# An FFT filter and a low-rank mixer on one core: x loaded as 128 partitions in runs of eight rows, chunk and natural stores in one DMA

## The chip, the cores and the metric

The kernel runs on one core of a Trainium2 chip. The metric is the device time of one execution in microseconds; lower is better. The core has five engines that run their own instruction streams and meet at semaphores: PE (matmuls; its weight loads are shown as PEld), DVE, ACT and POOL (element work), and SP, which here only issues DMAs. DMAs are moved by 16 DMA engines that all queues share. POOL issues on a software queue (q0 in the profile), SP and ACT on hardware queues (q1 and q10).

## The reference

```python
def _attn_ref(x, filt_r, filt_i):            # x: (8, 3136, 256) f32; filt: (1569, 256)
    X = np.fft.rfft(x, axis=1)
    Y = X * (filt_r + 1j * filt_i)[None]
    return np.fft.irfft(Y, n=x.shape[1], axis=1)

def _moe_ref(x, U, V, w_ch1, w_ch2):         # U: (3136, 32), V: (32, 3136)
    h = x.transpose(0, 2, 1) @ U @ V
    u = x + h.transpose(0, 2, 1)
    ch = np.maximum(u @ w_ch1, 0.0) @ w_ch2  # 256 -> 1024 -> 256
    return u + ch
```

The second takes the first's output as its x. Eight batches are independent of each other.

## The kernel before

**The transform.** A sequence of 3136 rows is taken as 64 x 49: row index = 49 q + r, with q from 0 to 63 (`NQ`) and r from 0 to 48 (`NR`). The first transform runs over q, on PE, with the constant matrix `w64` (two copies of a 64 x 64 block on the diagonal), so that partitions 0 to 63 handle one set of r and partitions 64 to 127 another. The 49 values of r are therefore held in 25 columns of two halves (`NH = 25`; the second half has 24). Which r stands in which half and column is a list, `r` in `_consts`: blocks of four, first half 0-3, 8-11, ..., second half 4-7, 12-15, .... A chunk of x (`CH = [8, 8, 9]` columns, `load_x`, L147 to L163) is a tile `xt` of 128 partitions, cast from f32 to f16 by the DMA. The second transform runs over r, with the table `t2` (its rows in the order of that list), then comes the product with the filters (`ft`), then the inverse over r with table `g12`, and the inverse over q.

**The stages of a batch.** Batch 0 stays in SBUF (`first_f1`, `first_a`, `first_mid`). The other seven go through DRAM twice: `f1_units` (L451 to L470) multiplies a chunk by `w64` into `asb` (L460, L466) and stores it to `c1[b]` (L470); `load_a` (L480, on SP) reads it back by frequency; `forward`, `product` and `i1` (in `stream`) do the second transform, the products (DVE, and the sum on POOL, L523) and the inverse over r, and store to `c2[b]`; `load_e` reads that back as `e2`. `make_u` forms u with the low-rank part, `mm1` and `mm2` are the two channel matmuls. A group is 4 columns of one batch, that is 8 rows r of 64 q.

**Outputs.** In batches 0 and 1 and in the last two groups of the last batch the result is evicted with positions on the partitions (`out_natural`, L733) into an `och` tile (2 buffers) and stored by L743, on POOL, in the last batch on SP. From batch 2 on it is evicted channel-major and turned by DVE (`out_turned`, L774, L775) and stored by eight DMAs (L783), four on SP and four on POOL. Every second batch an odd column is stored by L738.

**The order.** The order is written by hand: groups run one after another, each has eight slots, a batch has 48 (`SB`), and `put` places the units of the other stages into slots. For batches above 3 chunk c of x is loaded at slot t0 - 72 + 12c and its first transform unit comes at t0 - 54 + 12c, where t0 is the slot of the batch's first product; `load_a` of a batch stands at t0 - 14. Each engine runs its instructions in the order in which they were issued. POOL's queue holds x loads, c1 stores (batch 1's are on SP), POOL's part of the output stores, the sums of the products, and at the start the filters, tables, V and weights. POOL's DMAs take eight semaphores in turn, so that each waits for the landing of the eighth DMA before it. `xt` has five buffers.

Of the kernel before, what the change touches and what calls it, by code (L numbers as in the profile page):

```python
# [13 lines left out]
SEQ = 3136  # L14
NQ, NR = 64, 49
NS = 32
DM = 256
RANK = 32
ESC = 16.0
NH = 25  # L20
CH = [8, 8, 9]
# [5 lines left out]
def _consts():  # L27
    n, half = SEQ, SEQ // 2
    r = np.array([8 * (k // 4) + 4 * h + k % 4 for h in range(2) for k in range(NH - h)])
    q = np.arange(NQ)  # L30


    w = np.zeros((NQ, NS, 2))
    for s in range(NS):
        w[:, s, 0] = np.cos(2 * np.pi * s * q / NQ)
        w[:, s, 1] = -np.sin(2 * np.pi * s * q / NQ)
    w[:, 0, 1] = (-1.0) ** q
    w = w.reshape(NQ, 64)
    turn = np.arange(64).reshape(4, 16).T.ravel()
    w64 = np.zeros((128, 128))  # L40
    w64[:64, :64] = w
    w64[64:, 64:] = w
    s2 = np.zeros((128, 128))
    s2[:64, :64] = w.T / ESC
    s2[64:, 64:] = w.T / ESC


    t2 = np.zeros((NS, 98, 128))
    g = np.zeros((NS, 128, 98))
    for s in range(NS):  # L50
        for j in range(49):
            if j < 25:
                f = s + 64 * j
                e, sg = np.exp(-2j * np.pi * f * r / n), 1.0
            elif s:
                f = 64 * (j - 24) - s
                e, sg = np.exp(-2j * np.pi * (n - f) * r / n), -1.0
            else:
                f = 32 + 64 * (j - 25)
                e, sg = np.exp(-2j * np.pi * f * r / n), 1.0  # L60
            ei = np.conj(e)
            if s:
                t2[s, :49, j], t2[s, 49:, j] = e.real, -e.imag
                t2[s, :49, 64 + j], t2[s, 49:, 64 + j] = sg * e.imag, sg * e.real
                g[s, j] = np.concatenate([ei.real, ei.imag]) * 2
                g[s, 64 + j] = np.concatenate([-ei.imag, ei.real]) * 2 * sg
            else:
                o = 0 if j < 25 else 49
                t2[s, o:o + 49, j] = e.real
                t2[s, o:o + 49, 64 + j] = e.imag  # L70
                g[s, j, o:o + 49] = ei.real * (2 if f else 1)
                g[s, 64 + j, o:o + 49] = -ei.imag * 2

    t2[0, :, 64] = 0
    t2[0, 49:, 64] = (-1.0) ** r
    g[0, 64] = 0
    g[0, 64, 49:] = (-1.0) ** r
    g *= ESC / n
    gs = np.concatenate([g[:, 64:], g[:, :64]], 1)
    f16 = np.float16  # L80
    return (w64.astype(f16), s2.astype(f16), np.eye(128).astype(f16),
            np.tile(np.eye(32), (4, 4)).astype(f16),
            np.pad(np.hstack([w[:, turn], w[:, turn].T / ESC]), ((0, 64), (0, 0))).astype(f16),
            np.ascontiguousarray(t2.reshape(4, 8, 98, 128).transpose(0, 2, 1, 3)).astype(f16),
            np.ascontiguousarray(g.reshape(4, 8, 128, 98).transpose(0, 2, 1, 3)).astype(f16),
            np.ascontiguousarray(gs[0:8].transpose(1, 0, 2)).astype(f16))
# [3 lines left out]
def kernel(  # L90
# [11 lines left out]
    nc = tc.nc  # L102
# [10 lines left out]
    RD = NR * DM  # L113
    c1 = [nc.dram_tensor(f"c1_{b}", (64, RD), F16, kind="Internal") for b in range(nb)]
# [8 lines left out]
    def bank(tag, name):  # L123
        return ps.tile([128, 512], F32, tag=tag, bufs=BUFS[tag], name=name)

    c0 = np.cumsum([0] + CH).tolist()
    st = [dict() for _ in range(nb)]

    def span(lo, hi):

        for h in range(2):
            yield h, (h * NH + lo) * DM, (min(hi, NH - h) - lo) * DM

    def rows(ap, b, r, n):

        return bass.AP(tensor=ap.tensor, offset=ap.offset + (b * SEQ + r) * DM,
                       ap=[[RD, NQ], [1, n * DM]])

    def natural(ap):

        return ap.rearrange("p (r i h a) -> p r h i a", i=4, h=2, a=32)

    def split(ap):

        return ap.rearrange("p (r h i a) -> p r h i a", i=4, h=2, a=32)

    def load_x(b, c, parts=None):  # L147
        if c not in st[b].setdefault("x", {}):
            st[b]["x"][c] = sb.tile([128, 9 * DM], F16, tag="xt", bufs=5, name="xt")
        t = st[b]["x"][c]  # L150
        for lo, hi in parts or ((c0[c], c0[c + 1]),):
            for h in range(2):
                m = (hi - lo) // 4
                nc.gpsimd.dma_start(  # L154
                    t[64 * h:64 * h + 64, (lo - c0[c]) * DM:(lo - c0[c] + 4 * m) * DM]
                    .rearrange("p (m e) -> p m e", m=m),
                    bass.AP(tensor=x.tensor, offset=x.offset + (b * SEQ + 2 * lo + 4 * h) * DM,
                            ap=[[RD, NQ], [8 * DM, m], [1, 4 * DM]]))
            if hi == NH:
                o = (NH - 1 - c0[c]) * DM  # L160
                if b:
                    nc.gpsimd.memset(t[64:128, o:o + DM], 0.0)
                nc.gpsimd.dma_start(t[0:64, o:o + DM], rows(x, b, NR - 1, 1))  # L163
# [6 lines left out]
    t2 = cst.tile([98, NS * 128], F16)  # L170
# [62 lines left out]
    for c in range(1, len(CH)):  # L233
        load_x(0, c)
# [28 lines left out]
    for h in range(2):  # L263
# [3 lines left out]
                    ap=[[64 * 1024, 4], [1024, 32], [1, 1024]]))  # L267
# [183 lines left out]
    def f1_units(b, both):  # L451
        ne = 0
        for c in range(len(CH)):
            xt = st[b]["x"].pop(c)
            asb = sb.tile([128, 9 * DM], F16, tag="asb", bufs=2, name="asb")
            for n0 in range(0, CH[c], 2):
                w = min(2, CH[c] - n0) * DM
                k = 64 if c0[c] + n0 == NH - 1 else 128
                pf = bank("o" if b == 1 else "m", "pf")
                nc.tensor.matmul(pf[:, 0:w], w64[:, :], xt[:, n0 * DM:n0 * DM + w],  # L460
                                 start=True, stop=True)
                dst = asb[0:k, n0 * DM:n0 * DM + w]
                if both and (ne % 2 if b > 1 else ne > 3 and ne not in (5, 7, 12)):
                    nc.vector.tensor_copy(dst, pf[0:k, 0:w])
                else:
                    nc.scalar.copy(dst, pf[0:k, 0:w])  # L466
                ne += 1
                if n0 + 2 >= CH[c]:
                    for h, o, n in span(c0[c], c0[c + 1]):
                        (nc.sync if b == 1 else nc.gpsimd).dma_start(c1[b].ap()[:, o:o + n], asb[64 * h:64 * h + 64, 0:n])  # L470
                yield


# [254 lines left out]
    def out_natural(gx, rr):  # L728

        b, r0, nr = groups[gx]  # L730
        po, och = pos[gx], ochs[gx]
        a = (rr - rr % 2) * DM
        nc.vector.tensor_copy(natural(och[:, a:(rr + 1) * DM]), split(po[:, 0:(rr + 1) * DM - a]))  # L733
        if rr < nr - 1:
            return
        eng = nc.gpsimd if b < nb - 1 else nc.sync
        if nr == 1:
            eng.dma_start(bass.AP(tensor=out.tensor,  # L738
                                  offset=out.offset + ((b - 1) * SEQ + NR - 1) * DM,
                                  ap=[[SEQ * DM, 2], [RD, NQ], [1, DM]]), och[:, 0:DM])  # L740
        else:
            for h in range(2):
                eng.dma_start(rows(out, b, 2 * r0 + 4 * h, 4), och[64 * h:64 * h + 64, 0:nr * DM])  # L743

    def evict(gx, a):

        if gx < 0 or a >= groups[gx][2]:
            return
        if turned(gx):
            if a % 2:  # L750
                out_turned(gx, a)
        elif a % 2 or a == groups[gx][2] - 1:
            out_natural(gx, a)
# [57 lines left out]
    for h in range(2):  # L811
        nc.gpsimd.tensor_copy(split(w2)[:, :, h], natural(w2n)[:, :, h])
    fill = f1_units(1, True)
    vgen = u_units()
    first_mid(fill)
# [18 lines left out]
    for k, t in enumerate(steps):  # L834
        put(t, mid)
        b, m = divmod(k - LAG, NP)
# [8 lines left out]
    for b in range(1, nb):  # L845
        for gi in range(NS // KG):
            t = steps[NP * (b - 1) + GP * gi]
            put(max(2, t - (14 if b > 3 else 9 + b // 3)), one(load_a, b, gi))
        if b > 1:
            fill = f1_units(b, b == 2)  # L850
            t0 = steps[NP * (b - 1)]
            for k in range(NF):
                put(4 + 1.1 * k if b == 2 else 18 + 2.8 * k if b == 3 else t0 - 54 + 3 * k, fill)
            for c in range(len(CH)):
                if b > 2 or c > 0:
                    put(6 * c - 5 if b == 2 else 9 + 8 * c if b == 3 else t0 - 72 + 12 * c, one(load_x, b, c))
# [58 lines left out]
```

## Time and profile before

| | |
|---|---|
| median of 3 runs | 534.28 us (533.61 to 538.67) |
| the profiled execution | 534.16 us, span 532.4 us |
| PE / DVE / ACT / POOL busy | 498.4 / 400.7 / 377.7 / 290.9 us |
| granted PE clock, mean | 0.988 |
| x loads (L154) | 46 of 256 KB, median 6.7 us to landing; 4 of 128 KB, 3.9 us |
| c1 stores (L470) on POOL | 30 of 256 KB, 4.9 us; 6 of 288 KB, 3.7 us |
| natural output stores (L743) on POOL | 24 of 256 KB, 4.9 us |
| mean DMA rate | 177 GB/s |

The profile is of one execution. Times in it count from the start of its span. "Issue to landing" runs from the instruction that issues a DMA to its last completion step. Sizes of the x loads are those of the f16 that is written; twice as much is read.

### The profile page before, as it was taken

What the parts mean: (1) busy time and instruction counts of PE and PEld (TensorE: products, weight loads), DVE (VectorE), ACT (ScalarE), POOL (GpSimd) and SP (SyncE); (2) the same over time, 40 slices, a digit from 0 to 9 for tenths busy, and PEclk for the clock granted to TensorE, in tenths of its full rate; (3) what the DMA queues carried; (4) which work ended last, traced back from release to release, by engine and by line L of the source; (5) the groups of instructions that cost most, each with busy time, mean ns of one, the idle gap of its engine ahead of it and who ended that gap; (6) DMA issues with size and microseconds to landing.
All of it is one profiled execution on the core that took longest, in us unless ns stands there. A gap on an engine that the chain in (4) does not pass through costs nothing.

```text
span 532.4 us, 11368 instructions
## 1 busy us (share of the span) xinstructions
PE 498.4 (94%) x4022; PEld 303.0 (57%) x4022; DVE 400.7 (75%) x574; ACT 377.7 (71%) x771; POOL 290.9 (55%) x412
## 2 busy tenths in 40 slices
PE   3877799999999999999999999989999999999995
PEld 3765266667667785555555555545555555454444
DVE  7897367757786758898998888978999877445663
ACT  2767756677678868888788878877777678765541
POOL 7797633345656456586677665765756564313000
PEclk9979989999999999999999999999999999999999
DMA  8989998986988577897989798896887575544324
GB/s 127 193 150 188 204 211 210 217 223 147 232 234 214 141 154 221 208 229 171 225 204 220 195 240 205 177 235 145 199 194 148 126 180 128 140 96 80 78 66 104
DMA packets 118426, 93.98 MB, mean 177 GB/s; under 512 B 52977, under 2 KB 100786, under 8 KB 118370
## 3 DMA queue, kind: packets, MB, share of 16 engines
q0 software_dynamic: 21936, 41.91, 38.3%
q1 hardware_dynamic: 93226, 49.75, 37.7%
q10 hardware_dynamic: 3208, 1.61, 1.1%
q8 instruction: 31, 0.51, 0.4%
q14 instruction: 25, 0.20, 0.1%
HBM read 56.25 MB, written 48.17 MB: 196 GB/s over the span
## 4 chain that ended last, share of the span: by engine, by line
PE 79%; DVE 6%; POOL 6%; DMA 6%; issue 2%; ACT 1%; DVEq 0%; POOLq 0%; ACTq 0%
PE phh L694 27%; PE po L765 21%; PE po L720 8%; PE px L499 5%; PE pi L535 5%; PE pu L620 4%; DVE uv L520 3%; PE pf L460 3%; DMA xt<-in_x_dram 3%; PE ph L577 2%; POOL low L284 2%; DVE uv L518 1%; DMA vq<-in_moe_V_dram 1%; DMA g<-gd 1%; POOL xt L154 1%
## 5 line engine op out<-in xcount | busy, mean ns | idle before, releaser
L702 ACT ACTIVATE h<-phh 128x512 f16<-128x512 f32 (+1 forms) x391 | 205.9, 578 | 71.8 <-PE phh L694 66.9
L694 PE MATMUL phh<-ut,w 128*128 128x512 f16 x768 | 197.6, 379 | 0.6 <-ACT h L702 0.3
L523 POOL TENSOR_TENSOR y<-uv 128x512 f16<-128x512 f16 x96 | 111.0, 1158 | 110.6 <-DVE uv L520 74.8
L765 PE MATMUL po<-h,w 128*128 128x512 f16 x560 | 143.8, 379 | 0.0
L520 DVE TENSOR_TENSOR uv<-px,ft 64x512 f16<-64x512 f32 x192 | 132.1, 688 | 2.6
L694 PEld LDWEIGHTS <-w 128*128 128x128 f16 x832 | 78.5, 98 | 77.2 <-issue 2.4
L518 DVE TENSOR_TENSOR uv<-px,ft 128x512 f16<-128x512 f32 x96 | 65.3, 680 | 42.1 <-PE px L499 35.8
L783 POOL DMA_DIRECT2D out_dram<-och x120 | 70.2, 592 | 42.9 <-DVE och L775 35.6
L539 ACT CAST esb<-pi 98x512 f16<-98x512 f32 x112 | 66.0, 589 | 36.9 <-PE pi L535 33.9
L765 PEld LDWEIGHTS <-w 128*128 128x128 f16 x560 | 51.6, 98 | 53.2 <-issue 1.1
L774 DVE TENSOR_TENSOR tt<-po,ut 128x512 f32<-128x512 f32 x70 | 48.4, 692 | 33.8 <-PE po L765 30.9
L720 PE MATMUL po<-w,h 128*128 128x256 f16 x448 | 58.9, 275 | 0.0
L499 PE MATMUL px<-a,t 98*128 98x256 f16 x256 | 50.0, 277 | 7.2 <-DVE uv L520 3.7
L775 DVE STREAM_TRANSPOSE och<-tt 128x512 f32<-128x512 f32 x70 | 49.8, 711 | 2.4
L466 ACT CAST asb<-pf 128x512 f16<-128x512 f32 (+1 forms) x79 | 45.7, 578 | 5.3 <-PE pf L460 4.2
L720 PEld LDWEIGHTS <-h 128*128 128x128 f16 x448 | 42.8, 98 | 10.8 <-issue 1.4
L507 DVE TENSOR_TENSOR uv<-px,ft 128x1024 f16<-128x1024 f32 x32 | 38.0, 1219 | 13.9 <-PE px L499 13.4
L499 PEld LDWEIGHTS <-t 98*128 98x128 f16 x256 | 23.0, 99 | 33.9 <-DVE uv L520 11.5
L535 PE MATMUL pi<-y,g 128*98 128x256 f16 x192 | 36.7, 271 | 2.0 <-POOL y L523 2.0
L684 ACT CAST ut<-pu 128x512 f16<-128x512 f32 x70 | 38.1, 610 | 0.0
L460 PE MATMUL pf<-xt,w 128*128 128x512 f16 (+1 forms) x91 | 33.4, 373 | 3.3 <-DMA xt<-in_x_dram 3.0
L535 PEld LDWEIGHTS <-g 128*98 128x98 f16 x256 | 29.6, 123 | 4.0 <-issue 2.1
(96 smaller groups left out, 445.0 us busy)
## 6 DMA issues: line engine op xcount, KB each, us to landing
xt<-in_x_dram POOLq DMA_DIRECT2D x46, 256.0 KB, 6.7
a<-c SPq DMA_DIRECT2D x28, 384.0 KB
e<-c SPq DMA_DIRECT2D x56, 192.0 KB
out_dram<-och SPq DMA_DIRECT2D x160, 64.0 KB
c<-esb SPq DMA_DIRECT2D x24, 384.0 KB
c<-asb POOLq DMA_DIRECT2D x30, 256.0 KB, 4.9
out_dram<-och POOLq DMA_DIRECT2D x120, 64.0 KB, 3.2
out_dram<-och POOLq DMA_DIRECT2D x24, 256.0 KB, 4.9
```

The lines of the kernel that those rows point to most:

```text
L499: nc.tensor.matmul(px[:, sl * DM:(sl + 1) * DM], t2[:, s * 128:(s + 1) * 128], a2[:, (2 * ml + sl) * DM:(2 * ml + sl + 1) * DM], start=Tru ...
L518: nc.vector.tensor_mul(uv[:, 0:512], px[:, :], ft[:, a:a + 512])
L520: nc.vector.tensor_mul(uv[p:p + 64, 512:1024], px[q:q + 64, :], ft[q:q + 64, b:b + 512])
L523: nc.gpsimd.tensor_add(y, uv[:, 0:512], uv[:, 512:1024])
L535: nc.tensor.matmul(pi[0:98, sl * DM:(sl + 1) * DM], g12[:, g:g + 98], y[:, o:o + DM], start=(fi == 0), stop=(fi == nf - 1), skip_group_che ...
L539: nc.scalar.copy(split(esb[:, ml * 512:(ml + 1) * 512]), natural(pi[0:98, :]))
L694: nc.tensor.matmul(pm[:, 0:w], w1[:, dh * 1024 + t * 128:dh * 1024 + (t + 1) * 128], ut[:, dh * w:(dh + 1) * w], start=(dh == 0), stop=(dh ...
L702: nc.scalar.activation(h[:, 0:w], pm[:, 0:w], RELU)
L720: nc.tensor.matmul(po[:, o:o + DM], hs[gx, t][:, rr * 128:(rr + 1) * 128], w2[:, t * DM:(t + 1) * DM], start=(t == 0), stop=False, skip_gr ...
L765: nc.tensor.matmul(po[:, :], w2[:, t * DM + dh * 128:t * DM + (dh + 1) * 128], hs[gx, t][:, :], start=(t == 0), stop=(t == 7))
L775: nc.vector.transpose(och.rearrange("p (j h a) -> p h j a", h=2, a=32)[:, dh], tt.rearrange("p (j t) -> p j t", t=32))
L783: (nc.gpsimd if k and b < nb - 1 else nc.sync).dma_start(dst, och[32 * i:32 * i + 32, k * 512:(k + 1) * 512] .rearrange("p (r e) -> p r e" ...
```

## The change

`load_x` issues one DMA for a chunk of 128 partitions in place of two of 64. To make both halves of the tile one access pattern, the first half takes rows 0-7, 16-23, ... and the second 8-15, 24-31, ..., so that a partition reads one run of eight rows (8,192 bytes) in place of two runs of four. The forward table `t2` gets its rows in that order (`rf`); the inverse table keeps the old order. The c1 stores and the natural output stores of a chunk or group, two DMAs of 64 partitions so far, become one of 128. The DRAM side of all three has the dimensions (2, 64, n). The single last row of chunk 2 keeps a DMA of its own, in the load and in the store. Batch 0's first chunk is still loaded in two parts of four columns.

```diff
+    rf = np.array([16 * (k // 8) + 8 * h + k % 8 for h in range(2) for k in range(NH - h)])
...
+            fe = f if sg > 0 else n - f
+            e = np.exp(-2j * np.pi * fe * rf / n)
+            ei = np.exp(2j * np.pi * fe * r / n)
...
-    t2[0, 49:, 64] = (-1.0) ** r
+    t2[0, 49:, 64] = (-1.0) ** rf
...
-            for h in range(2):
-                m = (hi - lo) // 4
-                nc.gpsimd.dma_start(
-                    t[64 * h:64 * h + 64, (lo - c0[c]) * DM:(lo - c0[c] + 4 * m) * DM]
-                    .rearrange("p (m e) -> p m e", m=m),
-                    bass.AP(tensor=x.tensor, offset=x.offset + (b * SEQ + 2 * lo + 4 * h) * DM,
-                            ap=[[RD, NQ], [8 * DM, m], [1, 4 * DM]]))
+            n = min(hi, NH - 1) - lo
+            nc.gpsimd.dma_start(
+                t[:, (lo - c0[c]) * DM:(lo - c0[c] + n) * DM],
+                bass.AP(tensor=x.tensor, offset=x.offset + (b * SEQ + c0[c] + lo) * DM,
+                        ap=[[8 * DM, 2], [RD, NQ], [1, n * DM]]))
...
-                    for h, o, n in span(c0[c], c0[c + 1]):
-                        (nc.sync if b == 1 else nc.gpsimd).dma_start(c1[b].ap()[:, o:o + n], asb[64 * h:64 * h + 64, 0:n])
+                    eng, n = nc.sync if b == 1 else nc.gpsimd, min(8, CH[c]) * DM
+                    eng.dma_start(bass.AP(tensor=c1[b], offset=c0[c] * DM,
+                                          ap=[[NH * DM, 2], [RD, 64], [1, n]]), asb[:, 0:n])
+                    if CH[c] > 8:
+                        eng.dma_start(c1[b].ap()[:, (NH - 1) * DM:NH * DM], asb[0:64, n:n + DM])
...
-            for h in range(2):
-                eng.dma_start(rows(out, b, 2 * r0 + 4 * h, 4), och[64 * h:64 * h + 64, 0:nr * DM])
+            eng.dma_start(bass.AP(tensor=out.tensor, offset=out.offset + (b * SEQ + 2 * r0) * DM,
+                                  ap=[[4 * DM, 2], [RD, NQ], [1, 4 * DM]]), och[:, 0:nr * DM])
```

## The prediction

> **What bounds the kernel now.** I read the page's engine totals first, then the chain of work that ended last, then the DMA issues. PE is busy 94% of a span of 532.4 us; the other engines have air on average.
>
> ```profile
> span 532.4 us, 11368 instructions
> PE 498.4 (94%) x4022; PEld 303.0 (57%) x4022; DVE 400.7 (75%) x574; ACT 377.7 (71%) x771; POOL 290.9 (55%) x412
> ```
>
> So a DMA costs something only where PE ends up waiting for it. The chain in order of time (start, length, what) shows where that happens already: its DMA pieces of over 3 us all lie in the first 66 us, and two of the five are loads of x, which the change rewrites.
>
> ```profile
> 6.13 6.56 DMA xt<-in_x_dram
> ...
> 19.55 5.63 DMA g<-gd
> 28.50 3.10 DMA ft<-in_filt_r_dram
> 39.57 6.76 DMA vq<-in_moe_V_dram
> ...
> 58.70 7.32 DMA xt<-in_x_dram
> ```
>
> The question is then how long one of the new transfers takes. The DMA view from 38 to 56 us (issues, KB each, median us to landing) holds the nearest relative of the new access pattern:
>
> ```profile
> xt<-in_x_dram POOLq DMA_DIRECT2D x4, 256.0 KB, 6.7
> w<-in_moe_w_ch_dram POOLq DMA_DIRECT2D x2, 256.0 KB, 11.4
> ```
>
> Same queue, same bytes, same cast from f32, but the `w1` loads (L264) take 11.4 us against 6.7. Their DRAM side has a leading dimension of 4, (4, 32, 1024), against 128 SBUF partitions. The trace's completion records say why: each DMA reports 16 steps, one an engine. Those of an x load come together (41.1 to 42.5 us). Of the first `w1` load 12 come at 45.0 to 47.8 and four at 51.7 to 52.2: four engines carried its bytes, the others had nothing to do. The small `a` load (L480, two partitions) on SP also shows only two late steps.
>
> **The new transfers.** The x loads, the c1 stores and the natural output stores become DMAs whose DRAM side is (2, 64, n), where the two strides can't be merged: 8 rows against 49 rows times 64. By the `w1` row I take it that two engines carry each. This trace shows no such DMA of 128 partitions, so the bounds are 16 engines below (rival A) and two above. (The Trainium skill, DMA: Bandwidth & Descriptors, "Why a DMA increments its semaphore by 16 and not by 1", says that the number of engines is the largest up to 16 that divides the slowest dimension of both patterns: two here. By it the sum stays as below; the four of `w1` agree.)
>
> Price of an x chunk: the packet records give 172 ns in the median for a 2,048 B packet that reads 4,096 B of f32. A chunk is 128 runs of 8,192 B, so 64 an engine: 64 x 2 x 172 = 22.0 us. The fixed part is 2.0 us (the first load of the run is issued at 1.3 and completes at 4.0, with four packets in between). So **24 us** instead of about 7; at the mean of these packets between 205 and 340 us, 210 ns, it is 29. I take 24 where the queues are empty, 26 later. Several chunks can be under way on different pairs of engines.
>
> Price of a c1 store or a natural store of 512 KB: 64 x 172 ns = 11.0, with 2.5 for issue and landing 13.5 us, against 4.7 and 4.9; 16 at the packets' mean later on.
>
> **Start, through batch 2 (+55.8).** Batch 0's four x loads are issued at 1.3 to 5.2 us, so the last lands at 5.2 + 24 = 29.2 instead of 15.2. The first transform ends 1.8 us after that, as now. The filters and tables behind it share the two engines and POOL's waits for earlier DMAs, and are 14 late too; their own backlog (t2's first part takes 5.5 us to land now) is gone, so I take +12.5.
> x(1,0), issued at 32.6 + 12.5, lands at 69.1; PE reaches it at 40.7 + 12.5 = 53.2: a wait of 15.9, total 28.4. V, `w1` and `w2` queue behind the batch's chunks; x(1,2) lands at 73.5, so POOL's `low` copies move from 46.4 to 73.7 (+27.3), in step.
> x(2,0), 51.8 + 27.3, lands at 103.1, wanted at 59.5 + 28.4: a wait of 15.2, total 43.6. x(2,1), 58.1 + 27.3, lands at 109.4, wanted at 66.2 + 43.6: nothing. x(2,2) stands on POOL behind the c1 store of x(2,0), so is issued at 65.3 + 43.6 and lands at 132.9, wanted at 77.1 + 43.6: a wait of 12.2, total 55.8.
>
> **Batches 3 to 7 (+68).** From the issue (L154) and the first matmul on the chunk (L460) the leads are: batch 3: 17.8, 20.8, 25.8 us; 4: 22.0, 21.8, 18.1; 5: 19.8, 16.2, 16.3; 6: 16.5, 16.6, 16.4; 7: 19.1, 16.2, 16.7. Against 26 almost all are short. PE runs in order, so the chunk's first matmul holds everything. But POOL issues the second and third chunk of a batch shortly before PE reaches the one ahead (265.7 against 268.4), so a wait for one lengthens the next one's lead. Carried on in this way the waits are 5.2, 0 (batch 3, whose first chunk has batch 2's waits to hide in); 4.0, 0.2, 7.7; 6.2, 3.6, 6.1; 9.5, 0, 9.6; 6.9, 2.9, 6.4: 68 us. At 24 the same gives 50, at 29 it gives 95.
>
> **c1 store to `a` load (+25).** SP's `a` load (L480) waits for the last c1 store of its batch. The first load takes 6.1 us to land (61.8 to 67.9). From that store's issue to the first product of the batch there are now 18.9, 18.0, 14.1, 15.2, 13.7 and 14.7 us in batches 2 to 7; needed are 13.5 + 6.1 = 19.6: short by 0.7, 1.6, 5.5, 4.4, 5.9, 4.9, together 23; 32 at a store of 15 us. Batch 1's three stores are on SP, and if they share one pair they take 33 us in a row, which ends about when the late batch 2 chunk lets PE go on: 2 at most. Behind the waiting `a` load SP's output stores are late as well, and their buffers have 10 us to spare.
>
> **Outputs (+16, and +8 at the end).** Natural stores of batches 0 and 1: an `och` buffer is written again 9.4 to 20.7 us after its store; 13.5 us overshoot at two places, 6 us in all (0 to 20). Turned stores on POOL keep their form, but a part of each sits behind a chunk on its two engines, and POOL itself waits when the eighth DMA before has not landed: both end when the chunk does, where PE mostly waits anyway; 10 (0 to 30). At the end the one store of 512 KB follows the last full copy at 526.7: 526.7 + 0.5 + 2 + 11 = 540.3 instead of 532.4, so 7.9. Nothing hides it.
>
> **The clock (+15).** After PE's idle stretch of 2.4 us up to 29.2 the granted clock is half for 6.9 us (the view of stretches; after the busy times stand the clock, 0.51, DMA share and GB/s):
>
> ```profile
> 28.40:35.30 6.90, 6.00 (x53) 5.32 (x54) 6.76 (x8) 3.71 (x11) 6.82 (x12) 0.51 0.78 132
> ```
>
> Some 14 waits are longer than that; each may cost up to 3.4 us of PE, partly paid back by a longer lead for the next chunk: 15 (0 to 40).
>
> **What it saves.** 25 issues of x, 14 c1 stores and 13 output stores at 0.61, 0.55 and 0.54 us: about 30 us of POOL and SP. POOL is busy 55% and its longest waits are for DVE's products, so it frees nothing that PE waits for; at the start the second load goes out 1 us sooner and is lost in the 24. The reordered table (`rf`) changes constants only, the matmuls keep shape and count: 0.
>
> **Sum.** 532.4 + 55.8 + 68 + 25 + 16 + 7.9 + 15 = 720.1. The profiled execution took 534.16 for its span of 532.4, and the median of the runs is 534.28: with 1.8 outside the span **722 us**.
>
> **Rivals.**
> A, the other side: the new DMAs run on all 16 engines. Then a chunk's single DMA lands in about 5 to 7 us, and the saved issues shorten the start by the 1 us by which the second load is earlier, perhaps 3 with the x load at 58.7 on the chain: 530 to 535. It decides if the pattern is spread by its 128 rows and not by the leading 2; the output stores of the odd rows (also 128 rows, 4.4 us) do so, but their two strides merge into one. The four late steps of `w1` speak against it. (The Trainium skill, same page, "Rules for kernel authors", advises one 128-partition transfer instead of two over disjoint halves; that would be this rival, and no run of the trace before shows it.) 5%.
> B, two engines, but the slack hides the middle: POOL, held up less, issues its chunks earlier (by their slots the lead of batches 4 to 7 is 18 slots of about 1.3 us, 23 us), and the `a` loads overlap these waits. Then start, end and little else: 532 + 56 + 8 + 10 to 35 + 2 = 608 to 633. For it: POOL's lag of 7 us behind its slots is its own. Against: 23 is still below 26. 12%.
> C, two engines and a pile-up: contention with SP's queue makes a chunk 29 us or more, stores block POOL and y comes late. Start with four exposed loads 5 longer, 76, then 95 + 32 + 20 + 30 + 8 + 30: 825. 13%.
> Forecast: 70%.
>
> **Chances and range.** A comparison here can't tell a change of under 1% from none. Faster by over 1%: 2% (part of A). Within 1%: 3%. Slower: 95%. The low end takes 24 us in the middle (50), 15 for the `a` loads, no side costs, and 15 off for chunks that POOL issues earlier: 532 + 56 + 50 + 15 + 8 - 15 + 2 = 648, and I go a little into B, 640. The high end is near C's, 810.
>
> **What would show it.** Completion steps of an x load: 14 early, two some 20 us later; landing of xt about 24, of c1 stores about 13, of the last store about 13. PE idle before L460 by about 110 us in all, and half clock after it. Packets of x twice as large, half as many. If xt lands in under 10 us, the count of engines is wrong and with it everything; if it lands in 24 but PE's waits at L460 stay near the start's, B.

## The result and the profile after

The changed kernel takes **793.99 us** in the median of 6 runs (787.18 to 799.1), the kernel before 533.63 us in 6 runs beside it (530.93 to 538.67): a ratio of **1.4847 [1.4755, 1.494]**. The forecast was 722 us with a range of 640 to 810. The profiled execution took 795.25 us for a span of 793.5 us, 261.1 us more than the span before.

In the profile after, L454 is the first transform (L460 before), L464 the c1 store, L477 the `a` load (L480 before), L484 the `e` load (L487 before), L496 the second transform's matmul (L499 before), L739 and L780 the natural and the turned output stores. The page's totals and its row of granted clock:

```profile
span 793.5 us, 11290 instructions
PE 546.4 (69%) x4022; PEld 322.0 (41%) x4022; DVE 402.1 (51%) x574; ACT 382.9 (48%) x771; POOL 276.8 (35%) x363
PEclk9986876976987899869697786968769989999997
```

The work is the same: DVE and ACT are busy for 1.4 and 5.2 us more than before. PE was idle for 34.0 us and is now idle for 247.1. It is also busy for 48.0 us more, at a mean granted clock of 0.851 in place of 0.988. So 213.1 of the 261.1 us are idle time. The DMA issues of the page (KB each, median us to landing) say what has become slow. Before:

```profile
xt<-in_x_dram POOLq DMA_DIRECT2D x46, 256.0 KB, 6.7
...
c<-asb POOLq DMA_DIRECT2D x30, 256.0 KB, 4.9
out_dram<-och POOLq DMA_DIRECT2D x120, 64.0 KB, 3.2
out_dram<-och POOLq DMA_DIRECT2D x24, 256.0 KB, 4.9
```

After:

```profile
xt<-in_x_dram POOLq DMA_DIRECT2D x23, 512.0 KB, 24.5
...
c<-asb POOLq DMA_DIRECT2D x18, 512.0 KB, 15.9
out_dram<-och POOLq DMA_DIRECT2D x120, 64.0 KB, 4.7
out_dram<-och POOLq DMA_DIRECT2D x12, 512.0 KB, 18.0
```

Twice the bytes in one DMA take 3.2 to 3.7 times as long as the two halves took (6.7, 4.9 and 4.9 us). The turned stores, which the change leaves as they were, rise from 3.2 to 4.7. The completion records give the reason: of the chunk issued at 46.0 us 14 steps are in at 48.6 and the last two at 68.8. Two engines carry a merged DMA; the run `lead64` below tests it.

The chain that ended last, in order of time (start, length, what; nine of its DMA pieces of over 12 us):

```profile
5.91 23.77 DMA xt<-in_x_dram
...
79.82 22.67 DMA xt<-in_x_dram
...
111.82 25.15 DMA xt<-in_x_dram
...
162.19 21.52 DMA a<-c
...
269.06 22.88 DMA out_dram<-och
...
362.31 22.99 DMA a<-c
...
458.96 23.27 DMA a<-c
...
533.32 14.60 DMA c<-asb
...
566.74 24.31 DMA a<-c
```

Up to 137 us the long pieces are the chunks of x and V, which stands behind them on POOL. After that not one piece of over 10 us is a chunk. They are `a` and `e` loads, c1 and c2 stores and output stores, and the `a` load, which the change does not touch, has the largest share of all DMAs on the chain, 14% against 9% for x. PE's own groups say the same (busy, mean ns | idle before, and what ended most of it). Before:

```profile
L499 PE MATMUL px<-a,t 98*128 98x256 f16 x256 | 50.0, 277 | 7.2 <-DVE uv L520 3.7
...
L460 PE MATMUL pf<-xt,w 128*128 128x512 f16 (+1 forms) x91 | 33.4, 373 | 3.3 <-DMA xt<-in_x_dram 3.0
```

After:

```profile
L496 PE MATMUL px<-a,t 98*128 98x256 f16 x256 | 53.9, 296 | 123.8 <-DMA a<-c 76.1
...
L454 PE MATMUL pf<-xt,w 128*128 128x512 f16 (+1 forms) x91 | 38.4, 429 | 49.2 <-DMA xt<-in_x_dram 45.1
```

Ahead of the second transform PE was idle for 7.2 us and is now for 123.8; ahead of the first transform 3.3 and 49.2. Of those 45.1 us for x hardly any lie after 140 us; the same groups in the view of lines from 140 to 793 us:

```profile
L496 PE MATMUL px<-a,t 98*128 98x256 f16 x214 | 44.2, 290 | 120.0 <-DMA a<-c 75.5 <-issue 31.4 <-DVE uv L517 13.0
...
L454 PE MATMUL pf<-xt,w 128*128 128x512 f16 (+1 forms) x69 | 27.7, 402 | 8.6 <-DMA xt<-in_x_dram 8.3 <-DVE asb L458 0.3
```

The 31.4 us of "issue" belong to the `a` loads too: each of these four waits ends 0.1 us after an `a` load has landed. So in this stretch `a` loads end 106.9 us of PE's waits, in 11 pieces, and chunks of x 8.3 us. The `a` loads in question took 10.6 to 24.3 us from issue to landing.

SP's queue, with nearly the same instructions as before, waits longer too (us in all, times, longest). After:

```profile
SPq L484 <- DMA c<-esb: 101.0, 14, 21.3
...
SPq L477 <- DMA c<-asb: 83.1, 8, 41.3
```

The same two waits were 32.5 us (10 times, 7.4 at most) and 31.2 us (9 times, 10.4 at most) before.

**Where the time sits.** I compared the starts of the first matmul on each chunk and of the first matmul of the second transform in each quarter of a batch, which its first product needs, in the two traces. At the last chunk of batch 2 the new kernel is 60.0 us late. From there to the last batch's products the lag grows by 192.2 us: 145.8 of it is added at marks of first products, 46.4 at marks of first transforms. Of the 145.8, half (72 us) lies at the first quarters of batches 2 to 7, the rest nearly all at later quarters. A mark also takes in what PE lost on other work since the mark before it: 16.2 of the 46.4 come at the first chunk of batch 7, just after a wait of 14.9 us for the sum y. Behind them 8.9 are added, the most of it by the last store, issued at 779.0 and landing 13.0 us later. 60.0 + 192.2 + 8.9 = 261.1.

**How an untouched transfer gets late.** The `a` load issued at 362.3 us has 14 steps in at 366.3, and the other two at 385.3. Beside it is a chunk of x, issued at 359.5, landing at 383.6. In that stretch SP's packets of 512 B take 27 ns each and the chunk's of 4,096 B take 322. An `a` load has 384 KB, so 48 packets of 512 B an engine. If an engine that holds both queues takes them in turn, one for one, its share takes 48 x (0.322 + 0.027) = 16.8 us and some 3 us for issue and landing (the fastest `a` load of 8 KB takes 3.0), 20 in all (an estimate from these rows). The six slowest of the 28 `a` loads take 20.4 to 24.3 us, the fastest 3.9; the median is 9.7, where it was 5.0 before.

### The profile page after: what moved, and what is told of

Its sections match the earlier page's. It is cut to its first block, busy times and chain, and to the rows that moved or that the text cites. A ratio compares the mean times of both kernels' runs of the same rounds, so it can differ in the third digit from the quotient of the medians.

```text
span 793.5 us, 11290 instructions
## 1 busy us (share of the span) xinstructions
PE 546.4 (69%) x4022; PEld 322.0 (41%) x4022; DVE 402.1 (51%) x574; ACT 382.9 (48%) x771; POOL 276.8 (35%) x363
## 4 chain that ended last, share of the span: by engine, by line
DMA 43%; PE 36%; issue 8%; DVE 4%; POOL 4%; SPq 2%; ACT 0%; DVEq 0%; POOLq 0%; ACTq 0%
DMA a<-c 14%; PE phh L691 13%; PE po L762 11%; DMA xt<-in_x_dram 9%; DMA out_dram<-och 7%; DMA c<-asb 6%; DMA vq<-in_moe_V_dram 3%; PE po L717 3%; PE px L496 2%; DVE uv L517 2%; PE pi L532 2%; DMA c<-esb 2%; DMA e<-e 2%; PE pu L617 2%; PE pf L454 1%
## 5 line engine op out<-in xcount | busy, mean ns | idle before, releaser
L691 PE MATMUL phh<-ut,w 128*128 128x512 f16 x768 | 213.8, 403 | 5.8 <-ACT h L699 5.7
L762 PE MATMUL po<-h,w 128*128 128x512 f16 x560 | 153.8, 400 | 0.0
L496 PE MATMUL px<-a,t 98*128 98x256 f16 x256 | 53.9, 296 | 123.8 <-DMA a<-c 76.1
L691 PEld LDWEIGHTS <-w 128*128 128x128 f16 x832 | 82.4, 102 | 96.2 <-issue 28.2
L780 POOL DMA_DIRECT2D out_dram<-och x120 | 70.0, 591 | 67.5 <-DVE och L772 38.2
L496 PEld LDWEIGHTS <-t 98*128 98x128 f16 x256 | 23.7, 104 | 154.9 <-issue 81.4
L762 PEld LDWEIGHTS <-w 128*128 128x128 f16 x560 | 54.3, 102 | 60.0 <-issue 12.5
L454 PE MATMUL pf<-xt,w 128*128 128x512 f16 (+1 forms) x91 | 38.4, 429 | 49.2 <-DMA xt<-in_x_dram 45.1
L772 DVE STREAM_TRANSPOSE och<-tt 128x512 f32<-128x512 f32 x70 | 49.8, 711 | 44.1 <-DMA out_dram<-och 41.8
L460 ACT CAST asb<-pf 128x512 f16<-128x512 f32 (+1 forms) x79 | 45.4, 575 | 41.9 <-PE pf L454 40.7
L717 PE MATMUL po<-w,h 128*128 128x256 f16 x448 | 61.9, 284 | 2.0 <-DVE och L730 2.0
L532 PE MATMUL pi<-y,g 128*98 128x256 f16 x192 | 39.9, 291 | 14.9 <-POOL y L520 14.9
L532 PEld LDWEIGHTS <-g 128*98 128x98 f16 x256 | 32.9, 135 | 21.0 <-issue 18.1
## 6 DMA issues: line engine op xcount, KB each, us to landing
xt<-in_x_dram POOLq DMA_DIRECT2D x23, 512.0 KB, 24.5
c<-asb POOLq DMA_DIRECT2D x18, 512.0 KB, 15.9
```

Source lines behind the costliest of these rows:

```text
L496: nc.tensor.matmul(px[:, sl * DM:(sl + 1) * DM], t2[:, s * 128:(s + 1) * 128], a2[:, (2 * ml + sl) * DM:(2 * ml + sl + 1) * DM], start=Tru ...
L532: nc.tensor.matmul(pi[0:98, sl * DM:(sl + 1) * DM], g12[:, g:g + 98], y[:, o:o + DM], start=(fi == 0), stop=(fi == nf - 1), skip_group_che ...
L691: nc.tensor.matmul(pm[:, 0:w], w1[:, dh * 1024 + t * 128:dh * 1024 + (t + 1) * 128], ut[:, dh * w:(dh + 1) * w], start=(dh == 0), stop=(dh ...
L717: nc.tensor.matmul(po[:, o:o + DM], hs[gx, t][:, rr * 128:(rr + 1) * 128], w2[:, t * DM:(t + 1) * DM], start=(t == 0), stop=False, skip_gr ...
L762: nc.tensor.matmul(po[:, :], w2[:, t * DM + dh * 128:t * DM + (dh + 1) * 128], hs[gx, t][:, :], start=(t == 0), stop=(t == 7))
L772: nc.vector.transpose(och.rearrange("p (j h a) -> p h j a", h=2, a=32)[:, dh], tt.rearrange("p (j t) -> p j t", t=32))
```

## The experiments

In the kernels that start from the change, "halves" means that a DMA is cut at partition 64 again, each half with 64 rows outermost. Each has the runs of eight rows and the reordered table.

### The merging, undone: `halves`

All three merged DMAs cut again; the row order of the change stays.

```diff
-            nc.gpsimd.dma_start(
-                t[:, ...],
-                bass.AP(..., ap=[[8 * DM, 2], [RD, NQ], [1, n * DM]]))
+            for h in range(2):
+                nc.gpsimd.dma_start(
+                    t[64 * h:64 * h + 64, ...],
+                    bass.AP(..., ap=[[RD, NQ], [1, n * DM]]))
...
-                    eng.dma_start(bass.AP(tensor=c1[b], ..., ap=[[NH * DM, 2], [RD, 64], [1, n]]), asb[:, 0:n])
+                    for h in range(2):
+                        eng.dma_start(c1[b].ap()[:, ...], asb[64 * h:64 * h + 64, 0:n])
...
-            eng.dma_start(bass.AP(tensor=out.tensor, ..., ap=[[4 * DM, 2], [RD, NQ], [1, 4 * DM]]), och[:, 0:nr * DM])
+            for h in range(2):
+                eng.dma_start(rows(out, b, 2 * r0 + 4 * h, 4), och[64 * h:64 * h + 64, 0:nr * DM])
```

> The changed kernel with its three merged DMAs cut in two again, one for each half of 64 partitions; the runs of eight rows and the reordered forward table stay. Theory (the leading 2 of the merged DRAM patterns confines each DMA to two engines, and nothing else in the change matters): an x load lands in 5 to 8 us as before, with its 16 completion steps together, the granted clock is back near 0.99, and the time is that of the kernel before, 528 to 537 us. Rival (the longer runs of 8,192 bytes or the new row order are slow by themselves): x loads keep landing in over 12 us and the time stays above 600.

Measured: 535.1 us in 12 runs against 533.2, a ratio of 1.0027 [0.999, 1.0065]. Its DMA issues:

```profile
xt<-in_x_dram POOLq DMA_DIRECT2D x46, 256.0 KB, 6.5
...
c<-asb POOLq DMA_DIRECT2D x36, 256.0 KB, 4.5
```

The row order and the longer runs cost nothing that shows. All of the loss comes from the merging.

### Merged, with 64 outermost: `lead64`

Is it one DMA of 128 partitions that is slow, or the 2 that stands outermost? Here partition 2q + h holds half h of q, so the same bytes have the DRAM dimensions (64, 2, n). The first transform takes a constant with interleaved rows and columns (`wx`), the last row goes to the even partitions, and the whole of its column is cleared first. The natural stores are halves.

```diff
+    wx[0::2, 0::2] = w
+    wx[1::2, 1::2] = w
...
-                        ap=[[8 * DM, 2], [RD, NQ], [1, n * DM]]))
+                        ap=[[RD, NQ], [8 * DM, 2], [1, n * DM]]))
...
-                                          ap=[[NH * DM, 2], [RD, 64], [1, n]]), asb[:, 0:n])
+                                          ap=[[RD, 64], [NH * DM, 2], [1, n]]), asb[:, 0:n])
```

> x and c1 go in one DMA of 128 partitions each, as in the change, but partition p holds q = p // 2 and half p % 2, so that the DRAM pattern is (64, 2, n) instead of (2, 64, n); the first transform's constant matrix has its rows and columns in that order, the natural stores are in halves. Theory of the leading dimension: all 16 engines carry each DMA, an x load lands in 6 to 9 us, a c1 store in 4 to 6, and with one issue fewer for each chunk the time is 526 to 536 us, at or a little under the kernel before. Rival (one DMA of 128 partitions is slow whatever its dimensions are, for its size or for one queue's order): x still takes over 15 us and the time is over 600.

Measured: **529.96 us** in 9 runs, a ratio of **0.9936 [0.9913, 0.9959]**: the loss is gone. By the interval it is a little faster than before, but a gain of 0.6% is less than the 1% below which the prediction took a comparison here to tell nothing. Its issues:

```profile
xt<-in_x_dram POOLq DMA_DIRECT2D x23, 512.0 KB, 7.5
c<-asb POOLq DMA_DIRECT2D x18, 512.0 KB, 4.9
```

The same 512 KB land in 7.5 us where they took 24.5, and in 4.9 where they took 15.9. Queue, bytes, runs and the count of partitions are the same; what has changed is the order of the dimensions, and with it which partition holds which run. So the outermost 2 is the cause. (The Trainium skill, DMA: Bandwidth & Descriptors, "Why a DMA increments its semaphore by 16 and not by 1", gives the number of engines as the largest up to 16 that divides the slowest dimension of both patterns: two for (2, 64, n), 16 for (64, 2, n). The steps and both landings agree.)

### One part alone: `x_only`, `c1_only`, `out_only`

`x_only` takes the second and third hunk of `halves`, so only the loads of x are merged; `c1_only` the first and third; `out_only` the first and second.

```diff
 x_only: c1 and natural stores
+                    for h in range(2):
...
 c1_only: loads of x and natural stores
+            for h in range(2):
...
 out_only: loads of x and c1 stores
+            for h in range(2):
```

> Of the three merged DMAs only the x loads stay merged; c1 stores and natural stores are in halves. Theory: x lands in 23 to 27 us; start, waits at the first transform, the half clock after them, and a loads that are slow because a chunk's packets of 344 ns stand between theirs on two engines: 690 to 740 us, so that x alone makes most of the 261 us of span that the change adds. Rival (the three costs hang together, so that most of the loss needs the late c1 stores too): under 660.

> Of the three merged DMAs only the c1 stores stay merged; x loads and natural stores are in halves. Theory: a c1 store lands in 13 to 16 us, two of its 16 steps last; the a load that waits for a batch's last store comes later by some 9 us, which costs 23 to 45 us over the batches: 555 to 580. Rival (the x loads explain all of the loss, and the stores have slack enough): under 540.

> Of the three merged DMAs only the natural output stores stay merged. Theory: the store of 512 KB lands in 13 to 18 us; the last one of the run ends 8 us later than now, the twelve in batches 0 and 1 overshoot their buffers' slack a little, and they slow the a and e loads beside them: 545 to 565. Rival (only the end counts): 540 to 543.

Measured: `x_only` 779.19 us, 1.4623 [1.4567, 1.4679]; `c1_only` 645.49 us, 1.2084 [1.2018, 1.2149]; `out_only` 581.19 us, 1.0867 [1.081, 1.0924]. All three lie above what was expected. Alone they cost 246, 112 and 48 us, 406 together, and the three at once 260. The waits overlap: while PE waits for one, the others are late at no price. Merging the loads alone gives nearly all of the loss.

In `x_only` a chunk lands in 24.7 us, and the c1 stores and natural stores, which are halves there, take 8.5 and 13.8 us (4.5 and 4.6 in `halves`). They are issued on POOL behind the chunks. Its `a` loads take 11.1 us in the median and 25.2 at most.

In `c1_only` the first products of batch 1 are 34.8 us late. Batch 1's three c1 stores are on SP. They are issued at 45.3, 51.3 and 67.3 us and land at 62.7, 77.3 and 89.8, each with its last two steps late. The DMA view of that kernel from 30 to 120 us shows what they do to the machine (40 slices of 2.25 us: busy share of the 16 engines in tenths, and GB/s):

```profile
DMA  9789999996871111111492117996957210001717
GB/s 117 142 157 201 214 203 146 162 156 115 163 159 46 45 42 45 45 44 37 66 213 66 40 58 127 229 198 144 261 149 171 47 40 9 0 0 16 173 60 211
```

From slice 13 to 19 (57 to 73 us) the rate is 37 to 46 GB/s, and a tenth or so of the engines' time is used, as two of 16 would give. The stores end one behind the other, 14.6 and 12.5 us apart: these three share one pair of engines.

### Batch 1's stores apart: `c1_pool`

`c1_only` with batch 1's stores on SP in halves.

```diff
+                    if b == 1:
+                        for h in range(2):
+                            eng.dma_start(c1[b].ap()[:, ...], asb[64 * h:64 * h + 64, 0:n])
+                    else:
                         eng.dma_start(bass.AP(tensor=c1[b], ..., ap=[[NH * DM, 2], [RD, 64], [1, n]]), asb[:, 0:n])
```

> As the kernel in which only the c1 stores are merged, but batch 1's three stores, which go by SP, are in halves again. Theory (SP's merged stores use the same two engines one after the other, so that the last lands 22 us after its issue and batch 1's products start 35 us late): the offset at batch 1's first product falls from 35 to under 8 us, and the time from 645 to 600 to 618. Rival (the late POOL stores would hold the middle anyway): the time stays above 630.

Measured: 617.13 us, 1.1487 [1.1386, 1.1588]. The first products of batch 1 are 11.5 us late, above the 8 expected but 23 less than in `c1_only`, and the time is 28 us less. So the three serial stores cost some 28 us where nothing else hides them. In the full change the first product of batch 1 is 43.4 us late, and the two chunks of batch 2 that PE takes just before it are as late (43.0 and 43.8); with x alone it is 45.1. There the late chunks cover the stores.

### Shorter merged DMAs: `x_parts4`

`x_only`, a chunk as two merged DMAs of four columns.

```diff
-        for lo, hi in parts or ((c0[c], c0[c + 1]),):
+        for lo, hi in parts or ((c0[c], c0[c] + 4), (c0[c] + 4, c0[c + 1])):
```

> As the kernel in which only the x loads are merged, but a chunk is loaded as two DMAs of four columns each, both of 128 partitions with the leading 2: half the bytes for each DMA, packets that read 4,096 bytes instead of 8,192, and four engines in all for a chunk. Theory: each part lands in 13 to 15 us, inside most of the leads of 16 to 22; the start loses about 20 us instead of 56; an a load beside a chunk takes up to 13 us (48 packets, each behind one of 172 ns, plus 3) instead of 23: 560 to 600 us in all. Rival (software transfers ahead on an engine hold the hardware queue's packets until they end, in whatever packets they go): the a load beside a chunk ends only when the chunk's part ends, and the time is above 620.

Measured: 647.93 us, 1.219 [1.2139, 1.2242], a part landing in 15.2 us. The loss is 115 us where whole chunks cost 246. The time is above what the theory gave, and above the 620 that the rival named. The `a` loads take 15.3 us at most in place of 25.2, near the 13 of the theory; but the slow ones also end about when the parts beside them do, as the rival has it. This run does not decide between the two; `extra_small` below does. The two parts of a chunk run beside each other. At the last chunk of batch 2 it is 34.6 us late in place of 61.7.

### Transfers that nobody waits for: `extra_two`, `extra_sixteen`

If the middle is lost by what the long DMAs do to others, then they need no reader. Both kernels are the kernel before plus a copy of 512 KB (f16, from f32) to a scratch tensor behind each of the 15 chunk loads of batches 3 to 7. Nothing reads it. `extra_two` has the pattern of the change, `extra_sixteen` the same bytes in halves.

```diff
+    def load_more(b, c):
+        load_x(b, c)
+        t = nc.dram_tensor(f"spare_{b}_{c}", (128, 8 * DM), F16, kind="Internal").ap()
+        nc.gpsimd.dma_start(t[:, :], bass.AP(..., ap=[[8 * DM, 2], [RD, NQ], [1, 8 * DM]]))
...
 extra_sixteen
+        for h in range(2):
+            nc.gpsimd.dma_start(t[64 * h:64 * h + 64, :], rows(x, b, 16 * c + 8 * h, 8))
```

> The kernel before, with one extra copy of eight rows of x (512 KB written, f16) to a DRAM scratch behind the load of each chunk of batches 3 to 7, 15 copies; the DRAM pattern of its source is (2, 64, n), and nothing waits for the data. Theory (what costs in the middle is not PE waiting for a chunk, but every other transfer whose share lies on the same two engines: the a loads on SP, and the output stores behind it on POOL): a loads beside a copy take 15 to 25 us, and the time goes up by 60 to 150 us, to 595 to 685. Rival (the loss in the middle needs PE's own wait for the late chunk): under 560, only POOL's waits for the eighth DMA before showing.

> The same extra copies, each cut in two halves of 64 rows, which is spread over 16 engines: same bytes, 30 DMAs instead of 15. It measures what the bytes alone cost. Theory: a loads stay under 13 us, 534 to 548 us. Rival (the bytes are what costs, not the two engines): as much as with the merged copies.

Measured: `extra_two` **760.06 us**, 1.4173 [1.4066, 1.428]; `extra_sixteen` 554.09 us, 1.0374 [1.0293, 1.0454]. Both lie above what was expected, the first by far. The bytes and issues cost some 18 us, the two engines 206 more, and no engine computes on the result. That is about as much as the middle of the changed kernel (192), though a like size does not show that it has the same parts. Of `extra_two` the page's issues:

```profile
xt<-in_x_dram POOLq DMA_DIRECT2D x46, 256.0 KB, 6.6
...
c<-asb POOLq DMA_DIRECT2D x30, 256.0 KB, 15.8
spare<-in_x_dram POOLq DMA_DIRECT2D x15, 512.0 KB, 27.7
```

The loads of x, issued ahead of the copies, keep their 6.6 us. The c1 stores, on all 16 engines and unchanged, go from 4.9 to 15.8 us: they are issued behind the copies on POOL's queue, and two of their 16 engines are the copies'. On SP's queue it is as after the change:

```profile
SPq L487 <- DMA c<-esb: 128.2, 12, 23.9
```

Its `a` loads take up to 26.9 us.

### The same bytes in short packets: `extra_small`

If SP's loads wait packet for packet, then shorter packets of the copies should let them pass. The same two engines and bytes, in runs of 2,048 B of f32, so that a packet writes 1,024 B.

```diff
-                                             ap=[[8 * DM, 2], [RD, NQ], [1, 8 * DM]]))
+                                             ap=[[8 * DM, 2], [12 * DM, 256], [1, 2 * DM]]))
```

> The extra copies on two engines once more, the same bytes, but in runs of two rows: the DRAM pattern is (2, 256, 512), so that each engine has 256 packets that read 2,048 bytes instead of 64 that read 8,192. A copy still lands in 22 to 32 us. Theory (an engine that has work from POOL's queue and from SP's takes a packet from each in turn, so SP's transfer waits for as many of the other's packets as it has itself): the 48 packets that an a load has on an engine wait for packets of about 0.1 us instead of 0.34, and an a load beside a copy lands in 8 to 12 us instead of 20 to 27. POOL's output stores stay behind the copy in the same ring, so a part of the loss stays: 590 to 690 us. Rival (the other queue's transfer waits for the whole copy, or gets a fixed share of the time): a loads beside a copy still take 20 us and the time stays near 760.

Measured: 766.48 us, 1.4326 [1.4248, 1.4403]: no gain at all. But the transfers did as expected. The copies' packets take 96 ns, and an `a` load that has a copy beside it all the time takes mostly 9 to 12 us (7.1 at least, 14.2 at most), in place of up to 26.9. Issued early in a copy, it lands well before the copy does, so it does not wait for the whole of it. The loss came back at another place, POOL (its waits and DVE's):

```profile
DVE och L781 <- DMA out_dram<-och: 114.2, 8, 20.3
...
POOL out_dram L789 <- DMA spare<-in_x_dram: 95.0, 5, 24.6
```

In `extra_two` these are 60.6 and 46.0 us. The copies now land in 31.7 us, and POOL's DMAs, eight semaphores in turn, wait for them; the output stores behind them are late, and DVE waits for their buffers. So these times bear out that the packets of two queues alternate, and that alone does not set the time.

### Which queue: `extra_half_pool`, `extra_half_act`

Copies that read half as much (four rows; f32 to f32 without a cast, so that 512 KB are still written), once on POOL's queue, once on ACT's, to leave POOL's queue clear.

```diff
+        t = nc.dram_tensor(f"spare_{b}_{c}", (128, 4 * DM), F32, kind="Internal").ap()
+        nc.gpsimd.dma_start(t[:, :], bass.AP(..., ap=[[8 * DM, 2], [RD, NQ], [1, 4 * DM]]))
...
 extra_half_act
+        nc.scalar.dma_start(t[:, :], bass.AP(..., ap=[[8 * DM, 2], [RD, NQ], [1, 4 * DM]]))
```

> The extra copies of batches 3 to 7 once more, on POOL's queue and on two engines each, but half as large and without a cast: runs of four rows, 64 packets of 4,096 bytes an engine, 512 KB in all. It is the partner of the run with the same copies on ACT's queue. A copy lands in 13 to 18 us; the time goes up by 60 to 120 us, to 595 to 655, since both the a loads beside it and POOL's own stores behind it are late.

> The same half-size copies on two engines each, issued on ACT's queue instead of POOL's. Theory A (POOL's own queue is the heavier part: its later stores and loads lie behind the copy in the same ring, and POOL stands still at the eighth DMA): on a queue of their own the copies only share the two engines packet by packet, and the time goes up by less than half of what it does with the copies on POOL, to 545 to 580. Theory B (sharing the two engines with the a loads is the heavier part): the time goes up by nearly as much as with the copies on POOL.

Measured: on POOL 618.96 us, 1.1585 [1.154, 1.1629], on ACT 675.46 us, 1.2633 [1.2565, 1.27]. The first is as expected; the second lies above both theories. The expectation that a queue of its own would make the copies cheap falls. Of `extra_half_act`, SP's waits:

```profile
SPq L480 <- DMA spare<-in_x_dram: 72.4, 4, 18.4
SPq L789 <- DMA spare<-in_x_dram: 47.8, 3, 16.4
...
SPq L487 <- DMA spare<-in_x_dram: 34.3, 5, 16.5
```

SP does not read the copies. In the trace the DMAs of SP and ACT take the same eight semaphores in turn, so SP's `a` loads, stores and `e` loads wait until a copy from ACT has landed. (A copy issued at 272.9 us lands at 292.7, and SP's next store on its semaphore goes out at 292.7.) The pair therefore changes two things at once, the queue and the semaphores, and does not split the time between the order within POOL's queue and the sharing of packets. That split stays open. For POOL's own stores it does tell: with the copies on POOL's queue the c1 stores of 256 KB take 8.0 us and the natural stores 9.2, with the copies on ACT's 6.2 and 5.5 (4.9 and 4.9 without copies). And against `extra_two`, copies on POOL that read half as much, have no cast and land in 16.6 us cost 85 us in place of 224, which is less than half.

## Why the prediction was right, and where its sum was not

**The step that all hangs on held.** Two engines carry a merged DMA; 14 completion steps come early and two some 20 us later. x chunks take 24.5 us in the median (forecast 24, 26 later; 23.7 to 26.9 later on), c1 stores 15.9 (13.5 to 16). Natural stores on POOL take 18.0, above the 16; the last store takes 13.0. The packets of x are twice as large and half as many: 4,096 B in place of 2,048. Rival A, 16 engines, is what `lead64` is; it needs 64 outermost. (The Trainium skill, DMA: Bandwidth & Descriptors, "Rules for kernel authors", advises one 128-partition transfer in place of two over partition halves. Here that is right only with 64 outermost, 530.0 us with x and c1 merged against 535.1 in halves, and wrong with 2 outermost, 794.0. Another row of the same table asks for a multiple of 16 outermost, and that is the one that decides.)

| term of the sum | forecast | measured |
|---|---|---|
| start, through batch 2 | 55.8 | 60.0 |
| first transforms, batches 3 to 7 | 68 | 46.4 at these marks; PE waits 8.3 for x |
| c1 store to `a` load, batches 2 to 7 | 25 | 72 at first quarters; 145.8 with the later ones, which had no term |
| outputs | 16 | not apart from the marks; alone 48, with the end |
| end | 7.9 | 8.9 |
| clock | 15 | not apart; PE busy 48.0 more |
| span | 187.7 | 261.1 |

**Luck in the total.** That the time of 794 us lies in the range of 640 to 810 is in part luck: a term that was far too large (68 for x) partly made up for one that was far too small (25 for the `a` loads), and the upper end came from rival C, whose cause did not occur. The rise of the span is 261.1 us where 187.7 were forecast.

**Start: right, step by step.** Batch 0's last load lands at 29.7 (29.2 forecast), x(1,0) at 68.8 (69.1), x(2,0) at 102.5 (103.1), x(2,1) at 108.8 (109.4). Only x(2,2) is later, 137.0 against 132.9: it is issued at 111.8 and not 108.9, and takes 25.2 us and not 24.

**First transforms, +68: the step failed.** I took each chunk to be read as soon as PE comes to it, and PE to come on time. "PE idle before L460 by about 110 us in all" is 45.1 for x, at what is now L454, and 36.8 of it is in the start. PE is so late from other waits that the lead of 16 to 26 us between issue and use has grown to 25 to 48, mostly past the landing. Rival B had this outcome, by POOL issuing sooner; here it is PE that comes later. By the prediction's own sign, PE's waits for x near the start's, B would have held; but B kept 10 to 35 us for the rest, and its 633 us are far below what was measured.

**c1 store to `a` load, +25: the mis-sized term.** The step priced the late c1 store and kept the `a` load at the 6.1 us of a quiet stretch, though its 16 engines include the two that the chunk holds for 24 us. It takes up to 24.3 us, at a median of 9.7. PE waited 106.9 us for `a` loads after 140 us, about half of it at first quarters, where the late c1 store stands in front, and half at later quarters, for which the sum had nothing. What I had written of turned stores, that "a part of each sits behind a chunk on its two engines", holds for every transfer that is spread, on each queue. I charged it to one group on one queue, and at no more than PE waits anyway. `extra_two` shows the size of what was left out, for all transfers beside a copy together: 224 us with nothing waiting for the data, 206 of them from the two engines.

**Batch 1's stores on SP, "2 at most": right here, by the cover.** Alone they cost some 28 us; the late chunks hide them.

**Outputs, +16.** An och buffer has 9.4 to 20.7 us of room. I set 6 us for the natural stores at 13.5. Natural stores alone cost 48 us with the 8.7 of the end, so some 39 more than nothing where 6 were priced; and DVE's wait for an och buffer at L772 is 41.8 us in the changed kernel. How much of it ends up in the span there is not separated.

**Clock, +15.** PE is busy 48.0 us more at a granted clock of 0.851. Part of that may lie in stretches where PE would have waited; no run changes the clock alone, so its share stays open.

Rival C had the pile-up in its price (825), but for contention that makes a chunk slower; chunks take at most 26.9 us here, not the 29 or more that C needs. What piles up are the others.

**What stays open:** the middle's 192 us by cause. PE's waits for `a` loads are 106.9 us in it; what made each of these loads late is not split further. Order within POOL's queue, packets shared on SP's, and semaphores taken in turn each show in a run, and in `extra_small` the first took over where the second was eased.

## What to carry to other kernels

Read the outermost dimension of both sides of a DMA before you merge two into one: with 2 in front, 512 KB landed in 24.5 us here, with 64 in front in 7.5, and interleaving the partitions with a permuted constant was enough to get there, at no cost (ratio 0.9936). Price a long transfer on few engines by what it does to all the others, which need a piece from each engine: 15 of them, with nobody waiting for their data, cost 206 us more than the same bytes spread. Waits of this kind overlap and replace each other, so the parts do not add (406 us alone, 260 together).

## What the runs showed of the hardware that was not expected

- A DMA on SP with 2 outermost has three completion records, one 1 us after issue and two at the end. All three of batch 1's stores used the same pair of engines: 14.6 and 12.5 us apart, at 37 to 46 GB/s.
- Two queues at one engine are served in turn, by the estimate above as many packets of one as of the other: an `a` load with 48 packets an engine takes up to 24.3 us beside packets of 322 ns, and up to 14.2 beside packets of 96 ns. Whether they alternate singly or in small groups no run here shows. An `e` load with two packets an engine, issued at 241.2 us beside a chunk and with nothing of SP's ahead of it, lands in 6.0 us; `e` loads behind a slow `a` load or c2 store on SP's queue take up to 22.9.
- SP and ACT share eight DMA semaphores in this program, so that a slow DMA on ACT holds SP's issues (154.5 us of SP's waits in `extra_half_act`).
- Packets of 4 bytes on POOL's queue go from 5,768 to 54,264 with the change (5,864 in `halves`, 5,176 in `lead64`). They take 9 ns each. Without the 16 completion steps of each DMA, the change adds 55 x 14 x 64 of them for its 55 merged DMAs on POOL: as many as if each of the 14 engines without data took one for every run that a busy engine carries. The counts of `x_only`, `c1_only`, `out_only` and `extra_two` fit it exactly, and in `extra_small`, with 256 runs an engine, it is 14 x 256 for each copy. What they are for the trace does not say.
